# Attention, mixture of experts and a gated layer on one core: weight conversions taken off ScalarE, the closing of an expert from PSUM, twelve idle products for twenty-eight, and one more expert's weights loaded during attention

## The chip, the cores and the metric

The kernel runs on one core of one Trainium2 chip. Its time is the device time of one execution in microseconds; several executions are taken and their median is given. Engines are called as the profile calls them: TensorE (PE), VectorE (DVE), ScalarE (ACT), GpSimd (POOL) and SyncE (SP), which here does nothing but issue transfers.

## The reference

Three stages follow each other, with tokens as rows (1536 tokens, 512 columns).

```python
def _attn_ref(q, k, v):                 # (2, 8, 768, 64) each
    # every query sees keys at a distance under 16, and one summary key and value for each block of 32
    ...
def _moe_ref(x, w_skip, w_gate, w1, w2):      # 8 experts, 512 -> 1024 -> 512
    do_compute = x @ w_skip > 0               # the other tokens pass unchanged
    e_idx = np.argmax(xc @ w_gate, axis=1)    # one expert for each token
    ...
    h = np.maximum(xc[mask] @ w1[e], 0.0)
    y[mask] = gate_w[mask, None] * (h @ w2[e])
    out[do_compute] = xc + y
def _moe2_ref(x, w_in, w_out):                # 512 -> 2048 -> 512
    h = x @ w_in
    g = h * np.tanh(np.log1p(np.exp(h)))      # with a guard for h > 20
    return g @ w_out
```

The two weights of the last stage, `w_in` and `w_out`, arrive as 64-bit floats (two 32-bit words each) and are turned into 32-bit ones on the chip.

## The kernel before, in words

**Stages.** Attention runs over 24 groups of four 64-query tiles. In its last groups the gate's logits are summed, the tokens are ranked within their experts, and lists of row numbers are built. All token rows are written to `xd` in device memory; the last three stores of 512 KB come from `keep` (L775). Then follow the experts (L1077 to L1123), a branch for experts with many tokens that isn't taken with these inputs (L1136), and the last stage (from L1258), where TensorE alternates `up` (L989) and `down` (L1236) for 32 steps.

**Order.** The queues of SP and PE follow the order of the program text. On the other engines instructions stand in the order that a scheduler gave them, which in the expert loop and behind it is that of the text too.

**One expert.** GpSimd gathers up to 64 of its rows from `xd` (`fetch`, L855). The first product `g1_pair` (L892) puts the two halves of the hidden layer into partitions 0 to 63 and 64 to 127; ScalarE applies the relu; TensorE transposes the result (`flip`, L869); ScalarE copies it from PSUM (`hT`, L339); the second product `g2_pair` (L898) leaves two partial sums in one PSUM tile `yp`, again in the two halves of the partitions. The loop is staggered: the pass for expert e holds the first product of e and the second product of e - 1. `close_small` (L902) multiplies both halves by the gate and adds the token's row, and GpSimd writes the rows back to `xd` (`store`, L862). `yp` of these second products always comes from the same one of two PSUM buffers, since the branch for experts with over 64 tokens (`whole`, L1107) takes the other. So a second product can't begin before VectorE has closed the expert before. That branch is taken for experts 1 and 2.

**Weights of the experts.** Three sets of buffers are used in turn (`room`, L167): `big` for experts 0, 3 and 6, `raw` for 1, 4 and 7, `wb` (four buffers of `ring2`, which also held the values summed in attention) for 2 and 5. The loads of expert e + 2 stand in the pass of e, behind the second product of e - 1.

**Conversions.** `conv` (L118) turns one 128 x 512 piece of `w_in` or `w_out` into the two 32-bit parts that the last stage multiplies. ScalarE takes the absolute value of the high words (L127); six VectorE instructions follow (L129, L132, L135, L138, L113, L116). Ten of the 32 pieces are converted among the experts, `CONVS[e]` of them in the pass of e behind `close_small`; the tenth behind the branch at L1136. `conv_all` starts the next piece's ScalarE part while the present one is on VectorE, and the tile between them (`cv`) has two buffers. Four buffers hold raw pieces, so SP loads another when one has been converted.

**From the experts to the last stage.** After the last expert the rows are read back from `xd` in three transfers (`x_first`, L1125: 256, 512 and 768 KB), and they wait for the last store. TensorE meanwhile runs 28 products whose results nothing reads (`stir`, L1260); then it transposes the rows (`x_turn`, L1165), ScalarE rounds them (L1170), VectorE takes the remainder (L1171), and the last stage starts.

Of the kernel before, what the change touches and what calls it, by code (L numbers as in the profile page):

```python
# [15 lines left out]
ALU = mybir.AluOpType  # L16
# [12 lines left out]
def kernel(  # L29
# [87 lines left out]

    def conv(hi, low_, raw, hi_eng):  # L118
        t = cvp[0].tile([P, 512], F32, tag="cv", name="cv")
# [3 lines left out]
        else:  # L123
            words = raw.rearrange("p a b -> p (a b)").rearrange("p (f w) -> p f w", w=2)
            low, high = words.bitcast(U32)[:, :, 0], words.bitcast(U32)[:, :, 1]
            tu = t.bitcast(U32)
            nc.scalar.activation(out=t, in_=words[:, :, 1], func=AF.Abs)  # L127
            yield
            nc.vector.tensor_scalar(out=t, in0=t, scalar1=_f32(0x38000000), scalar2=_f32(0x47EFFFFF),  # L129
# [515 lines left out]
    LAG0 = N // 2 + 4  # L645
    RAW_AT = 17
    WAIT = [("w1", 0, kk) for kk in range(KD)] + [("w2", 0, kk) for kk in range(KD)]
    WAIT += [("w1", 1, kk) for kk in range(KD)] + [("w2", 1, kk) for kk in range(KD)]
    FEED_AT = dict(zip((7, 8, 10, 11, 13, 14, 16, 17), (2, 1) * 4))
    for i in range(-4, N - 3):  # L650
# [71 lines left out]
        if i == RAW_AT:  # L722
# [3 lines left out]
            spool.append(rctx.enter_context(tc.tile_pool(name="rawp", bufs=4, side="right", reuse_waits="tile")))  # L726
        if i >= RAW_AT + 3 and WAIT:
            load(WAIT.pop(0))
# [172 lines left out]
    def close_small(e, yp):  # L901
        gt, xt = gtl[0:HT, 0, e:e + 1], xtile[e]  # L902
        yo = mo.tile([P, DM], F32, tag="yo", name="yo")[0:HT]
        nc.vector.scalar_tensor_tensor(out=xt[0:HT], in0=yp[0:HT], scalar=gt, in1=xt[0:HT], op0=ALU.mult, op1=ALU.add)  # L904
        nc.scalar.copy(yo, yp[HT:P])  # L905
        nc.vector.scalar_tensor_tensor(out=yo, in0=yo, scalar=gt, in1=xt[0:HT], op0=ALU.mult, op1=ALU.add)
        store(first_ids(e), yo)
# [110 lines left out]
    def conv_all():  # L1018
        begun = []

        def begin():
            key = SEQ[len(begun)]
            gen = conv(*seat(key), raws[key], nc.vector)
            if WIDE:
                next(gen)
            begun.append((key, gen))

        for n in range(len(SEQ)):
            if n == len(begun):
                begin()  # L1030
            key, gen = begun[n]
            for at, _ in enumerate(gen):
                yield False
                if at == 2 and n + 1 < len(SEQ) and SEQ[n + 1] in raws and SEQ[n + 1] != ("out", NH):
                    begin()
            raws.pop(key)
            if n >= EARLY:
                load_next()
            yield True
# [20 lines left out]
    for _ in range(NCVR - 1):  # L1060
        load_next()
    for nm in ("w1", "w2"):
        for kk in range(KD):
            load((nm, 2, kk))
    for e in range(2, E):
# [12 lines left out]
    done = 0  # L1078
    CONVS = (0, 1, 2, 2, 1, 1, 1, 1)
    for e in range(E):  # L1080
# [39 lines left out]
    yp = acc_y()  # L1120
    g2_pair(E - 1, hT, yp)
    close_small(E - 1, yp)
    def x_loads(dst, s, c):  # L1123
# [10 lines left out]

    x_first()
    with tc.If(regs[E] > CUT):  # L1136
        enroll()
# [15 lines left out]
        x_first()  # L1153
    for _ in range(EARLY - done):
        go_conv()
    mctx.close()
# [101 lines left out]
    stir = fps.tile([P, 512], F32, tag="acc0", name="stir", bufs=1)  # L1258
    for _ in range(28):
        nc.tensor.matmul(stir, wi[0, 0][:, 0, 0, 0:P], wi[0, 0][:, 0, 0, :], start=True, stop=True)  # L1260
    xs[0] = [h_[:, c, :] for h_ in holds for c in range(CB)]
# [10 lines left out]
    for c, tag in enumerate(("acc4", "acc5", "h")):  # L1272
        x_halves(x_turn(xs[0][c], tag), xts[0], c)
    rest = list(enumerate(("h", "acc2", "acc3"), 3))
# [76 lines left out]
```

## Time and profile before

| | us |
|---|---|
| median of three runs | 529.85 |
| the three runs | 533.31, 527.6, 529.85 |
| profiled execution, its own time | 530.17 |
| profiled execution, span | 527.9 |
| TensorE busy | 479.5 (91%) |
| VectorE busy | 328.9 (62%) |
| ScalarE busy | 294.1 (56%) |
| GpSimd busy | 78.1 (15%) |

Times in the profile count from the span's start. Attention takes up to about 120 us, the experts run from 124.57 to 237.66, and the first product of the last stage that runs on without a longer pause starts at 251.73. A row of the timeline gives the start, the duration, the engine, the line and the operation with the tile that it writes and those that it reads; in brackets stands how long the engine had been idle and what ended that. `PEclk` is the granted clock of TensorE, 1.00 for 2.4 GHz and 0.50 for 1.2 GHz.

### The profile page before, as it was taken

Reading aid. Unit: us, or ns where it says so; the run is one execution under the profiler, and the core shown is the slowest. Engines: PE = TensorE matmul, PEld = TensorE weight load, DVE = VectorE, ACT = ScalarE, POOL = GpSimd, SP = SyncE. Lnnn points to the kernel's source line nnn. Section 1 sums busy time; section 2 is a strip of 40 time slices with the busy share of each in tenths; the row PEclk is TensorE's granted clock in tenths of the full one; section 3 lists DMA queues with packets and bytes.
Section 4 is the critical chain, followed back from the end, with each engine's and each line's share of the span. In section 5 each row is a group of like instructions: output and inputs, shape, how many; then the busy total and the mean of one; then the engine's idle time right before and its main releaser. Section 6 shows DMA issues by size and latency. Waiting matters only on the chain.

```text
span 527.9 us, 7985 instructions
## 1 busy us (share of the span) xinstructions
PE 479.5 (91%) x2818; PEld 377.3 (71%) x2818; DVE 328.9 (62%) x811; ACT 294.1 (56%) x477; POOL 78.1 (15%) x122
## 2 busy tenths in 40 slices
PE   4888979876999969967899999999999999999996
PEld 2777968762344323325898989999899998989985
DVE  3776847755012375563489888987888878454434
ACT  2687958520122132322597786866767677585660
POOL 5765532306211211100000000000000000000000
PEclk9999979876999998997999999999999999999999
DMA  8899999456998469943041221212212100030003
GB/s 182 220 215 213 232 243 296 127 195 208 371 400 305 174 225 402 389 177 126 1 160 44 78 69 51 79 45 76 77 44 81 40 1 0 1 119 1 1 0 119
DMA packets 58146, 76.41 MB, mean 145 GB/s; under 512 B 23950, under 2 KB 36286, under 8 KB 57712
## 3 DMA queue, kind: packets, MB, share of 16 engines
q1 hardware_dynamic: 56432, 73.95, 44.4%
q0 software_dynamic: 1664, 1.83, 1.2%
q8 instruction: 26, 0.43, 0.3%
q14 instruction: 24, 0.20, 0.1%
HBM read 70.76 MB, written 7.96 MB: 149 GB/s over the span
## 4 chain that ended last, share of the span: by engine, by line
PE 48%; DVE 4%; ACT 2%; issue 0%; DVEq 0%; ACTq 0%
PE acc L1236 23%; PE hp L989 22%; PE stir L1260 2%; PE ptx L1165 1%; DVE big L1228 1%; DVE big L1217 1%; DVE xt L1171 0%; DVE big L1205 0%; ACT big L1213 0%; DVE big L1225 0%; ACT big L1209 0%; ACT big L1202 0%; DVE wo L116 0%; DVE cv L135 0%; DVE ot L1251 0%
## 5 line engine op out<-in xcount | busy, mean ns | idle before, releaser
L989 PE MATMUL hp<-xt,wi 128*128 128x384 f32 x768 | 140.1, 336 | 2.4 <-ACT xt L1170 1.6
L989 PEld LDWEIGHTS hp<-xt,wi 128*128 128x128 f32 x768 | 134.5, 188 | 5.6 <-ACT xt L1170 2.0
L1236 PE MATMUL acc<-wo,big 128*128 128x512 f32 x576 | 138.2, 392 | 0.0
L1236 PEld LDWEIGHTS acc<-wo,big 128*128 128x128 f32 x576 | 107.2, 188 | 20.9
L1202 ACT ACTIVATE big<-hp 128x384 f32<-128x384 f32 x64 | 31.3, 492 | 65.7 <-PE hp L989 65.6
L1217 DVE TENSOR_TENSOR big<-big 128x768 f32<-128x768 f32 x32 | 30.6, 957 | 33.6 <-ACT big L1213 33.6
L1205 DVE COPY big<-hp 128x384 f32<-128x384 f32 x64 | 35.5, 556 | 23.3 <-ACT big L1202 23.3
L1213 ACT ACT_TABLE_LOAD x32 | 41.1, 1283 | 0.6
L1202 ACT ACT_TABLE_LOAD x31 | 39.8, 1283 | 0.6
L1228 DVE TENSOR_TENSOR big<-big 128x768 fp32r<-128x768 f32 x32 | 30.7, 959 | 3.1
L413 ACT ACTIVATE pr<-pr,nb 128x120 f32<-128x120 f32 x96 | 30.0, 386 | 1.1 <-DVE nb L407 0.9
L1213 ACT ACTIVATE big<-big,turn 128x768 f32<-128x768 f32 x32 | 30.1, 940 | 0.4
L917 DVE SCALAR_TENSOR_TENSOR yo<-yp,gtl,xs 128x512 f32<-128x512 f32 x2 | 1.5, 751 | 46.0 <-PE yp L929 46.0
L391 PE MATMUL sps<-kw,qb 128*128 128x120 f32 x192 | 28.2, 294 | 2.0 <-DVE qb L341 1.4
L391 PEld LDWEIGHTS sps<-kw,qb 128*128 128x128 f32 x192 | 25.8, 209 | 3.4 <-issue 2.4
L437 PE MATMUL xp<-vw,pts 120*64 120x65 f32 x384 | 21.2, 249 | 7.2 <-POOL vw L105 7.1
L1209 ACT ACTIVATE big<-big 128x768 f32<-128x768 f32 x32 | 27.1, 847 | 1.0
L127 ACT ACTIVATE cv<-raw 128x512 f32<-128x512 f32 x32 | 21.1, 663 | 9.8 <-DVE wi L116 7.3
L437 PEld LDWEIGHTS xp<-vw,pts 120*64 120x64 f32 x384 | 17.1, 153 | 11.1 <-POOL vw L105 8.1
L905 ACT COPY yo<-yp 64x512 f32<-64x512 f32 x8 | 4.7, 582 | 36.2 <-DVE xr L904 36.2
L424 ACT COPY pts<-tp 120x512 f32<-120x512 f32 x23 | 13.5, 585 | 18.2 <-PE tp L419 18.0
L135 DVE SCALAR_TENSOR_TENSOR cv<-raw,cv 128x512 uint32<-128x512 uint32 x32 | 22.2, 693 | 1.1
(182 smaller groups left out, 656.5 us busy)
## 6 DMA issues: line engine op xcount, KB each, us to landing
big<-in_moe_w_dram SPq DMA_DIRECT2D x24, 512.0 KB, 8.6
raw<-in_moe_w_dram SPq DMA_DIRECT2D x24, 512.0 KB, 8.3
raw<-in_moe_w_in_dram SPq DMA_DIRECT2D x16, 512.0 KB, 3.6
wb<-in_moe_w_dram SPq DMA_DIRECT2D x16, 512.0 KB, 8.0
raw<-in_moe_w_out_dram SPq DMA_DIRECT2D x16, 512.0 KB, 3.3
vw<-in_v_dram SPq DMA_DIRECT2D x16, 240.0 KB, 7.8
kr<-in_k_dram SPq DMA_DIRECT2D x16, 192.0 KB, 3.3
qr<-in_q_dram SPq DMA_DIRECT2D x16, 192.0 KB, 4.6
```

Of the source, the lines that this page charges most:

```text
L135: nc.vector.scalar_tensor_tensor(out=tu, in0=low, scalar=29, in1=tu, op0=ALU.logical_shift_right, op1=ALU.bitwise_or)
L391: nc.tensor.matmul(sps[:, j, :], qb[:, t].rearrange("p h i -> p (h i)"), kw[:, t, 0:NK], start=True, stop=True)
L413: nc.scalar.activation(out=pr[:, j, :], in_=pr[:, j, :], func=AF.Exp, bias=nb[:, j:j + 1], scale=SCALE)
L437: nc.tensor.matmul(xv[o0:o0 + QT, j // 2, h, :], pt[:, j, h * QT:(h + 1) * QT], vw[:, t, h, VP - D - 1:VP], start=True, stop=True)
L989: last_up[0] = nc.tensor.matmul(ps_, l(a), r(b_), start=(kk == 0 and n == 0), stop=(kk == KD - 1 and n == 2))
L1202: nc.scalar.activation(out=part(ds[n], half), in_=hps[n, half], func=AF.Sigmoid, scale=-1.0)
L1205: nc.vector.tensor_copy(part(us[n], half), hps.pop((n, half)))
L1209: nc.scalar.activation(out=d, in_=d, func=AF.Arctan)
L1213: nc.scalar.activation(out=d, in_=d, func=AF.Sin, scale=-2.0, bias=turn2)
L1217: nc.vector.tensor_tensor(out=u, in0=u, in1=part(ds[n], half), op=ALU.mult)
L1228: nc.vector.tensor_tensor(out=g_part(n, 1, half), in0=part(us[n], half), in1=g_part(n, 0, half).bitcast(F32), op=ALU.subtract)
L1236: nc.tensor.matmul(accs[t], g[:, a, t * P:(t + 1) * P], wo[f // 2][:, b_, f % 2, :], start=(n in FIRST and m == 0), stop=(n in LAST and m ...
```

## The change

1. `conv` gets a parameter `apart_`. Without it (the first ten pieces) the sign bit is cleared by one more VectorE instruction in place of ScalarE's; the next piece isn't started early. The other 22 pieces are converted as before.
2. `CONVS` becomes (0, 2, 2, 2, 1, 1, 1, 0). The tenth piece's instructions up to its rounding stand ahead of the last `close_small`, its last one behind it and ahead of the branch.
3. `close_small` reads the second half of `yp` from PSUM in its VectorE instruction; ScalarE's copy goes.
4. `stir`: 8 products, and 4 more behind the first transposes, for 28.
5. The eight loads of expert 2 join the list `WAIT` of loads in attention. That list is emptied faster: 1, 2, 3 and 4 loads at the ends of groups 17 to 20, where one stood at group 20; the buffers of `raw` open two groups earlier. What is left goes behind the three last stores to `xd`.

```diff
-    def conv(hi, low_, raw, hi_eng):
+    def conv(hi, low_, raw, hi_eng, apart_):
...
-            nc.scalar.activation(out=t, in_=words[:, :, 1], func=AF.Abs)
-            yield
+            if apart_:
+                nc.scalar.activation(out=t, in_=words[:, :, 1], func=AF.Abs)
+                yield
+            else:
+                nc.vector.tensor_scalar(out=tu, in0=high, scalar1=0x7FFFFFFF, scalar2=None, op0=ALU.bitwise_and)
...
-    RAW_AT = 17
+    RAW_AT = 15
...
+    WAIT += [("w1", 2, kk) for kk in range(KD)] + [("w2", 2, kk) for kk in range(KD)]
...
-        if i >= RAW_AT + 3 and WAIT:
+        for _ in range(max(0, i - RAW_AT - 1)):
             load(WAIT.pop(0))
...
-        nc.scalar.copy(yo, yp[HT:P])
-        nc.vector.scalar_tensor_tensor(out=yo, in0=yo, scalar=gt, in1=xt[0:HT], op0=ALU.mult, op1=ALU.add)
+        nc.vector.scalar_tensor_tensor(out=yo, in0=yp[HT:P], scalar=gt, in1=xt[0:HT], op0=ALU.mult, op1=ALU.add)
...
-            gen = conv(*seat(key), raws[key], nc.vector)
-            if WIDE:
+            gen = conv(*seat(key), raws[key], nc.vector, len(begun) >= EARLY)
+            if WIDE and len(begun) >= EARLY:
                 next(gen)
...
-                if at == 2 and n + 1 < len(SEQ) and SEQ[n + 1] in raws and SEQ[n + 1] != ("out", NH):
+                if at == 2 and EARLY <= n + 1 < len(SEQ) and SEQ[n + 1] in raws and SEQ[n + 1] != ("out", NH):
...
-    for nm in ("w1", "w2"):
-        for kk in range(KD):
-            load((nm, 2, kk))
...
-    CONVS = (0, 1, 2, 2, 1, 1, 1, 1)
+    CONVS = (0, 2, 2, 2, 1, 1, 1, 0)
...
     g2_pair(E - 1, hT, yp)
+    run(cv, 4)
     close_small(E - 1, yp)
...
     x_first()
+    go_conv()
...
-    for _ in range(EARLY - done):
-        go_conv()
...
-    for _ in range(28):
-        nc.tensor.matmul(stir, wi[0, 0][:, 0, 0, 0:P], wi[0, 0][:, 0, 0, :], start=True, stop=True)
+    def stir_on(n):
+        for _ in range(n):
+            nc.tensor.matmul(stir, wi[0, 0][:, 0, 0, 0:P], wi[0, 0][:, 0, 0, :], start=True, stop=True)
+
+    stir_on(8)
...
-        x_halves(x_turn(xs[0][c], tag), xts[0], c)
+        pt = x_turn(xs[0][c], tag)
+        if c == 0:
+            stir_on(4)
+        x_halves(pt, xts[0], c)
```

Three places show how instructions move. First ScalarE from the closing of expert 1, at the end of the pass of expert 2, on (the `hT` there is what the second product of expert 2 multiplies, in the pass of expert 3), before:

```order
130 L1107 UNCONDITIONAL_BRANCH x2
131 L905 COPY yo<-yp 64x512
132 L127 ACTIVATE cv<-raw 128x512 x2
133 L339 COPY hT<-pt 128x512
134 L885 ACTIVATE hr<-hp 128x512
135 L339 COPY xT<-pt 128x256
```

and with the change, at the same place:

```order
128 L1107 UNCONDITIONAL_BRANCH x2
129 L342 COPY hT<-pt 128x512
130 L889 ACTIVATE hr<-hp 128x512
131 L342 COPY xT<-pt 128x256
132 L1073 TENSOR_LOAD cnti
133 L1107 COMPARE_AND_BRANCH
```

Behind the branch `hT` now comes first; the copy `yo` and the two absolute values `cv` are gone from ahead of it.

Second, VectorE at the closing of the last two experts, up to the branch (`xr` and `yo` are the closing, `cv` and `wo` a conversion), before:

```order
498 L904 SCALAR_TENSOR_TENSOR xr<-yp,gtl,xr 64x512
499 L906 SCALAR_TENSOR_TENSOR yo<-yo,gtl,xr 64x512
500 L129 TENSOR_SCALAR cv<-cv 128x512
501 L132 TENSOR_SCALAR cv<-cv 128x512
502 L135 SCALAR_TENSOR_TENSOR cv<-raw,cv 128x512
503 L138 SCALAR_TENSOR_TENSOR cv<-raw,cv 128x512
504 L113 CAST wo<-cv 128x512
505 L116 TENSOR_TENSOR wo<-cv,wo 128x512
506 L904 SCALAR_TENSOR_TENSOR xr<-yp,gtl,xr 64x512
507 L906 SCALAR_TENSOR_TENSOR yo<-yo,gtl,xr 64x512
508 L1136 COMPARE_AND_BRANCH
```

and with the change:

```order
513 L908 SCALAR_TENSOR_TENSOR xr<-yp,gtl,xr 64x512
514 L909 SCALAR_TENSOR_TENSOR yo<-yp,gtl,xr 64x512
515 L131 TENSOR_SCALAR cv<-raw 128x512
516 L132 TENSOR_SCALAR cv<-cv 128x512
517 L135 TENSOR_SCALAR cv<-cv 128x512
518 L138 SCALAR_TENSOR_TENSOR cv<-raw,cv 128x512
519 L141 SCALAR_TENSOR_TENSOR cv<-raw,cv 128x512
520 L113 CAST wo<-cv 128x512
521 L908 SCALAR_TENSOR_TENSOR xr<-yp,gtl,xr 64x512
522 L909 SCALAR_TENSOR_TENSOR yo<-yp,gtl,xr 64x512
523 L116 TENSOR_TENSOR wo<-cv,wo 128x512
524 L1138 COMPARE_AND_BRANCH
```

The conversion has one instruction more and its last one stands behind the last closing; before, another whole conversion followed behind the branch.

Third, SP's queue at the end of attention (`vw` are values of attention, `raw` and `wb` the weights of experts 1 and 2, `xd<-xb` the last three stores of rows), before:

```order
84 L292 DMA vw_121<-in_v_dram 96x10x64
85 L293 DMA vw_121<-in_v_dram 80x64
86 L294 DMA vw_121<-in_v_dram 80x64
87 L199 DMA raw<-in_moe_w_dram 128x2x512
88 L775 DMA xd<-xb_117 128x2x512 x3
89 L199 DMA raw<-in_moe_w_dram 128x2x512 x3
90 L199 DMA raw<-in_moe_w_in_dram 128x1024 x4
91 L199 DMA wb<-in_moe_w_dram 128x1024 x4
92 L199 DMA wb<-in_moe_w_dram 128x2x512 x4
```

and with the change:

```order
85 L295 DMA vw_121<-in_v_dram 96x10x64
86 L296 DMA vw_121<-in_v_dram 80x64
87 L297 DMA vw_121<-in_v_dram 80x64
88 L202 DMA raw<-in_moe_w_dram 128x2x512 x3
89 L202 DMA wb<-in_moe_w_dram 128x1024 x4
90 L202 DMA wb<-in_moe_w_dram 128x2x512 x2
91 L779 DMA xd<-xb_117 128x2x512 x3
92 L202 DMA wb<-in_moe_w_dram 128x2x512 x2
93 L202 DMA raw<-in_moe_w_in_dram 128x1024 x4
```

Nine loads of 512 KB now stand between the last values and the three stores, where one stood.

## Rows read from the trace of the kernel before

**Rows 1.** The page: gigabytes per second in 40 slices of 13.2 us.
```profile
GB/s 182 220 215 213 232 243 296 127 195 208 371 400 305 174 225 402 389 177 126 1 160 44 78 69 51 79 45 76 77 44 81 40 1 0 1 119 1 1 0 119
```

**Rows 2.** Stretches: length, busy us of PE, PEld, DVE, ACT, POOL; PEclk, DMA share, GB/s.
```profile
97.00:109.00 12.00, 10.06 (x104) 9.01 (x103) 7.24 (x44) 5.27 (x14) 0.56 (x2) 0.64 0.26 67
199.50:203.60 4.10, 4.10 (x12) 0.98 (x8) 0.79 (x2) 0.00 (x0) 0.00 (x0) 0.59 1.02 417
240.30:243.80 3.50, 3.50 (x8) 2.78 (x9) 3.31 (x6) 1.19 (x2) 0.00 (x0) 0.50 0.64 203
300.00:350.00 50.00, 50.00 (x258) 45.40 (x256) 43.74 (x73) 38.41 (x47) 0.00 (x0) 1.00 0.21 71
```

**Rows 3.** Timeline, passes of experts 2 to 7: start, us, engine, line, tiles, [idle before].
```profile
155.19 1.94 PE L892 MATMUL hp<-wb,xT 128*64 128x512 f32 x8
...
181.49 0.66 PE L869 MATMUL pt<-ident,hr 128*128 128x128 f32 x4
...
186.12 0.67 ACT L127 ACTIVATE cv<-raw 128x512 f32<-128x512 f32 x1 [3.66 <-DVE wi L116]
...
187.46 3.65 PE L898 MATMUL yp<-wb,hT 128*64 128x512 f32 x16 [3.05 <-ACT hT L339]
...
198.25 5.35 PE L898 MATMUL yp<-big,hT 128*64 128x512 f32 x16 [2.02 <-ACT hT L339]
...
221.31 1.94 PE L892 MATMUL hp<-raw,xT 128*64 128x512 f32 x8 [0.31 <-PEq L1107]
```

**Rows 4.** Timeline, VectorE in the pass of expert 2: closing, then a conversion.
```profile
180.40 0.73 DVE L904 SCALAR_TENSOR_TENSOR xr<-yp,gtl,xr 64x512 f32<-64x512 f32 x1
...
182.57 0.41 DVE L129 TENSOR_SCALAR cv<-cv 128x512 f32<-128x512 f32 x1
...
185.40 0.69 DVE L116 TENSOR_TENSOR wi<-cv,wi 128x512 fp32r<-128x512 f32 x1
186.00 0.42 DVE L129 TENSOR_SCALAR cv<-cv 128x512 f32<-128x512 f32 x1
```

**Rows 5.** Timeline from the closing of expert 6 to the last stage.
```profile
229.92 0.74 DVE L904 SCALAR_TENSOR_TENSOR xr<-yp,gtl,xr 64x512 f32<-64x512 f32 x1 [3.18 <-PE yp L898]
...
230.59 3.65 PE L898 MATMUL yp<-raw,hT 128*64 128x512 f32 x16 [0.72 <-PEq L1107]
...
235.53 0.74 DVE L904 SCALAR_TENSOR_TENSOR xr<-yp,gtl,xr 64x512 f32<-64x512 f32 x1
...
236.92 0.74 DVE L906 SCALAR_TENSOR_TENSOR yo<-yo,gtl,xr 64x512 f32<-64x512 f32 x1 [0.65 <-ACT yo L905]
237.94 0.90 POOL L862 DMA_INDIRECT xd<-yo,idl  x1 [4.58 <-DVE yo L906]
...
240.22 2.18 SPq L1125 DMA_DIRECT2D big<-xd  x3
240.25 0.43 DVE L129 TENSOR_SCALAR cv<-cv 128x512 f32<-128x512 f32 x1 [2.59 <-DVEq L1136]
...
240.30 8.27 PE L1260 MATMUL stir<-wi 128*128 128x512 f32 x28 [6.06 <-DVEq L1136]
...
248.41 1.48 PE L1165 MATMUL ptx<-ident,big 128*128 128x128 f32 x12
...
251.73 1.14 PE L989 MATMUL hp<-xt,wi 128*128 128x384 f32 x5 [0.51 <-DVE xt L1171]
```

**Rows 6.** Transfers by line: KB each, median us from issue to landing.
```profile
big<-xd SPq DMA_DIRECT2D x1, 768.0 KB, 6.6
...
big<-xd SPq DMA_DIRECT2D x1, 256.0 KB, 3.1
```

**Rows 7.** Timeline, end of attention: SP's issues and the first gather.
```profile
97.29 0.43 SPq L199 DMA_DIRECT2D raw<-in_moe_w_dram  x1
...
109.23 3.96 SPq L775 DMA_DIRECT2D xd<-xb  x3
...
120.68 1.05 POOL L855 DMA_INDIRECT xr<-xd,idl  x1 [23.11 <-DVE gtp L581]
```

## The prediction

> **What bounds the kernel now.** I read the stretches first, then the timeline from the experts to the last stage. In the last stage TensorE is busy 50.00 of 50 us at a clock of 1.00 [rows 2], and the chain of waits from 251.73 on runs mostly through TensorE: what comes earlier there ends earlier, one for one. The questions are therefore when TensorE begins that stage and what held it back. Three places do. Twice a second product of an expert waits for `hT`: 3.05 us at 187.46 and 2.02 us at 198.25 [rows 3]. The transposes for the first wait had ended at 181.49 + 0.66 = 182.15; ScalarE was held at 186.12 by an absolute value that waited 3.66 us for VectorE to free a `cv` buffer, and `hT` stood behind it in the queue. The product at 198.25 then took 5.35 us where its like at 187.46 took 3.65, since the clock fell (0.59 in that stretch) [rows 2, 3]. Third, between the last second product's end, 230.59 + 3.65 = 234.24, and the last stage at 251.73 lie 17.5 us: closing, store, branch, 28 idle products of 8.27 us, transposes [rows 5]. The eight products in 240.30 to 243.80 ran at 0.50 [rows 2]; 28 cost 8.27, so the other 20 took about 4.8.
>
> **Experts.** The waits go with ScalarE's part: 3.05 + 2.02 = 5.07. Without the pauses I expect the clock not to fall there: 5.35 - 3.65 = 1.70. Together 6.77. ScalarE's copy of `yo` (the 0.65 us that VectorE waited at 236.92 [rows 5]) also leaves every closing; only the last lies on the path.
>
> In exchange VectorE gets longer. A conversion takes 186.00 - 182.57 = 3.43 us [rows 4]. The new instruction isn't in this trace: the nearest rows are a one-source instruction at 0.41 and a two-source one at 0.69 [rows 4]. It has one source and a constant, so I take 0.41, with its gap 0.45, and 0.69 as upper end. Two conversions become 7.76 us. What is late next is the closing, and behind it the next second product, which needs `yp`. The closing of expert 1 starts at 180.40; two dependent instructions of about 0.74 and the follow-on gap bring the conversions to 181.85 and their end to 189.6. Then come a count's load and a branch on VectorE; TensorE paid 0.72 us for both at 230.59 [rows 5], which I take, and the upper end is the 2.59 that VectorE spent at the far branch [rows 5]. Closing of expert 2: 190.3 to 191.8; TensorE wants `yp` at 198.25 - 5.07 = 193.2. Again two conversions and a branch: closing of expert 3 ends at 201.7. Without waits the two second products lie 198.25 - 187.46 - 2.02 = 8.8 apart [rows 3], so TensorE wants `yp` again at 202.0. That fits by a hair; I charge 0.3. **Experts: -6.5.**
>
> The freed DMA time gains nothing by itself: the first product of expert 2 started at 155.19 behind the product before it, with no wait for weights [rows 3]. Later loads follow their buffers, so they move up with TensorE, and SP's raw pieces wait for conversions as before. From the end of expert 2's second product, 187.46 - 3.05 + 3.65 = 188.1, until the last piece of expert 7's first weights 9.4 MB must arrive (18 pieces). At 389 GB/s, one of the fullest slices among the experts [rows 1], that takes 24.2 us, till 212.3; the product wants its first piece at 221.31 - 6.5 = 214.8 [rows 3]. Just covered; no charge.
>
> **Attention.** Nine loads (4.7 MB) now go out from 97.3 on [rows 7], in 12 us whose DMA share was 0.26 [rows 2]. They land beside work that needs no transfer. The three stores at 109.23 stand behind them, and the first gather at 120.68 needs both the stores and VectorE's lists [rows 7]. At 389 GB/s nine loads take 12.1 us, so they are through at 109.4: charge 0, bounds 0 and +1.5. The trace has no store queued behind loads. The Trainium skill, "DMA: Bandwidth & Descriptors", section "Queues, rings and completion order", says that each DMA engine takes the descriptors of one ring in order. By that the stores wait for the whole rest of the loads, which at 389 GB/s is next to nothing; no row here shows it. What a low rate would do is a rival below.
>
> **Closing.** Let expert 6's second product end at 229.9, as before. VectorE closes it, 229.92 to 231.4. The tenth conversion's first six instructions take 0.45 and 185.40 - 182.57 = 2.83 [rows 4]: until 234.6, just later than TensorE's 234.24. The last closing then runs without ScalarE, to 236.1; before it ended at 236.92 + 0.74 = 237.66 [rows 5]. So the store goes 1.5 us earlier (1.25 if the new instruction takes 0.69). The rows' transfers started 2.28 behind the store (237.94 to 240.22): now 238.7. The rest of the conversion, 0.69 [rows 4], now stands ahead of the branch: end 236.8. The branch took 2.59 from VectorE's last end to 240.25, and `stir` started right behind it [rows 5]; now 239.4. That is 0.9 earlier than 240.30, not 1.5.
>
> **Idle products.** Eight at the low clock, 0.43 each as in 240.30 to 243.80 [rows 2], end at 242.85. The first rows are there at 238.7 + 3.1 = 241.8; if they needed the 6.6 us of the large transfer [rows 6], 245.3, so this is bounded by +2.5. The transposes start 5.55 earlier than at 248.41. From there to 251.73 it took 3.3 us [rows 5]; the four products (0.21 each at the full clock) delay the second and third transposes and so ScalarE, 0.6. **Closing and idle products: -5.55 + 0.6 = -5.0.** The bulk of it is the 4.8 us of products at the full clock; it holds if the full clock has come by the time the eight are through.
>
> **Sum.** 530.17 - 6.5 - 5.0 = **518.7 us**. The profiled execution stands 0.3 above the median of 529.85, and the three runs spread over 5.7, so I don't correct for that.
>
> **Rivals.**
>
> *VectorE becomes the bound among the experts.* For it: the hair above, and a branch price that the trace doesn't show for a late VectorE. At 0.69 and 2.59 the conversions end at 190.1, the closing of expert 2 at 194.2 (+1.0), the one of expert 3 at 206.5, 3.5 behind TensorE. Against it: TensorE paid only 0.72. It costs up to 4.5: 519 to 522.9.
>
> *The clock doesn't hold.* With fewer products the low clock may reach into the last stage, or fall again while TensorE waits for ScalarE and VectorE, now about 1.7 us in one piece. For it: after a wait of 2.02 it fell at 199.5. Against it: after 3.05 at 187.46 it didn't, nor in the pauses before 251.73. One stretch of 3.5 us at 0.50, as at 240.30 [rows 2], loses 1.7, two lose 3.5: 520.4 to 522.2. The Trainium skill, "TensorE: Matmul & The Clock Gate", section "HAM oscillation", says that waits between bursts let the clock fall, so that every burst starts low. By that rule both prices fall due, 522.2; the trace agrees only after some of its waits, so this rival has no more than its chance.
>
> *The loads hold back the gathers.* In attention the busy slices moved 182 to 243 GB/s [rows 1]. Loads and stores are 6.3 MB from 97.3 on. At 243 they end at 123.2, the first gather is 3 us late: 521 to 522. At 182 they end at 131.9, 11.2 later than 120.68, and the gain is gone but for 0.3. Below 181 the change is **slower**; that is the point which decides. At 127, the lowest slice there, they end at 146.9: 530 to 545. Against it: those slices were full of small pieces, while weights alone moved at 371 and more.
>
> *The waits turn into waits for weights.* The cover of 2.5 us at expert 7 is thin; at 305 GB/s, the slower slice there [rows 1], the last piece comes at 218.9, 4.1 late: up to 522.8. Against it: the pieces come and are wanted one by one, and that slice held pauses of the queue.
>
> *It doesn't do what it says.* If `hT` is late for a reason other than ScalarE's queue, only the -5.0 is left: 525.2, within 1%. Little speaks for it, since the absolute value ends and `hT` starts 0.03 later.
>
> **How the numbers follow.** Forecast 0.48, VectorE 0.16, clock 0.14, gathers a little late 0.07 and so late that it gets slower 0.04, weights 0.06, not as said 0.05. Own range of the forecast: 516 to 521.5. The range of 515 to 524.5 takes in the rivals except the last of the gathers and of "not as said", and a run's scatter below. A measurement of this kernel can tell about 1% from no change, so faster means under 524.55: the first three, the late gathers and the weights, 0.91, less 0.06 for two of them at once: 0.85. Slower by over 1% (gathers at under 158 GB/s): 0.03. Within: 0.12.
>
> **What would show it.** In the changed profile the second products of experts 2 and 3 start right behind TensorE's work, without a wait for ScalarE; VectorE's closing of expert 3 ends about when TensorE needs it; the first gather still starts near 120.7; the last store leaves 8 us earlier than at 237.94; eight `stir` products run at 0.50 and the four later ones at 1.00; the steady stretch of the last stage begins near 240.2. Wrong would be: a late first gather, a wait of a second product for VectorE of more than 1 us, a clock of 0.50 behind the transposes, or a wait for rows.

## The result, and the profile after

The changed kernel took 527.11 us (median of 20 runs, 519.33 to 532.21), the kernel before 531.51 on the same chip (20 runs): ratio 0.9899, interval 0.9865 to 0.9933. That is 5.4 us or 1% faster, where 11.5 us were forecast. Ratios below leave disturbed runs out, so they can differ a little from the quotient of two medians. The profiled execution took 527.98, span 526.2; the changed kernel was profiled twice more, as f4 and k3 below.

First the experts. The rows of after that answer to [rows 3] (timeline, TensorE):

```profile
138.05 5.35 PE L902 MATMUL yp<-big,hT 128*64 128x512 f32 x16 [1.89 <-issue]
...
188.63 3.65 PE L902 MATMUL yp<-wb,hT 128*64 128x512 f32 x16
197.33 3.65 PE L902 MATMUL yp<-big,hT 128*64 128x512 f32 x16
...
218.99 2.27 PE L896 MATMUL hp<-raw,xT 128*64 128x512 f32 x8 [0.61 <-DMA raw<-in_moe_w_dram]
```

Both waits for ScalarE are gone, and the product that took 5.35 takes 3.65; the clock of 200 to 225 rose from 0.94 to 1.00. But there is a new wait for weights at expert 7, and a wait early on, at 138.05, that no step spoke of. VectorE in the pass of expert 2, after (answers to [rows 4]):

```profile
186.28 0.41 DVE L131 TENSOR_SCALAR cv<-raw 128x512 uint32<-128x512 uint32 x1
...
194.51 0.74 DVE L908 SCALAR_TENSOR_TENSOR xr<-yp,gtl,xr 64x512 f32<-64x512 f32 x1
```

The new instruction takes 0.41. Two conversions fill 186.28 to 194.37 (8.09 us, where the prediction took 7.76), the closing follows 0.14 later and ends before TensorE wants it at 197.33.

The end of the experts, after (answers to [rows 5]), and two rows of SP's waits (what waited <- what released it, us in total, times, longest), of after and then, by itself, of before:

```profile
228.79 3.65 PE L902 MATMUL yp<-raw,hT 128*64 128x512 f32 x16 [0.76 <-PEq L1107]
...
234.95 1.11 POOL L866 DMA_INDIRECT xd<-yo,idl  x1 [4.00 <-DVE yo L909]
236.60 1.28 ACT L1271 ACT_TABLE_LOAD   x1 [4.27 <-ACTq L1138]
237.84 1.54 SPq L1126 DMA_DIRECT2D big<-xd  x3
...
238.09 3.57 PE L1262 MATMUL stir<-wi 128*128 128x512 f32 x8 [5.64 <-ACT warm L1271]
243.69 0.66 PE L1165 MATMUL ptx<-ident,big 128*128 128x128 f32 x4 [2.03 <-SPq L1138]
...
248.00 2.69 PE L992 MATMUL hp<-xt,wi 128*128 128x384 f32 x6 [0.68 <-ACT xt L1170]
```

```profile
SPq L1138 <- SPq L1138: 4.2, 1, 4.2
```

```profile
SPq L1136 <- SPq L1136: 4.6, 1, 4.6
```

Counted from the start of the last second product, the store leaves at 6.16 us instead of 7.35 and the eight products start at 9.30 instead of 9.71. (What held them last, by their row, was ScalarE's first work behind the branch, `warm`, and not VectorE.) Then TensorE waits 2.03 us. Not for a transfer: for SP's branch (SPq L1138). SP issues the three row loads, 237.84 to 239.38, comes to the last branch and spends 4.2 us there; TensorE goes on at once (239.38 + 4.2 = 243.6). Before, the same row stood at 4.6: 242.40 + 4.6 = 247.0, and the 28 products lay over it until 248.57.

Stretches of after: length, busy us by engine, then PEclk, DMA share, GB/s.

```profile
234.30:241.60 7.30, 3.51 (x8) 2.49 (x8) 0.97 (x2) 1.49 (x2) 1.11 (x1) 0.53 0.52 158
241.80:244.80 3.00, 1.11 (x7) 1.03 (x8) 0.00 (x0) 0.29 (x1) 0.00 (x0) 0.99 0.73 246
244.90:251.20 6.30, 5.59 (x20) 4.40 (x19) 2.07 (x3) 1.36 (x3) 0.00 (x0) 0.50 0.01 3
```

The clock came to 1.00 when the eight products were through, and the first four transposes still ran at it (0.66). From 244.9 on it was 0.50 again, and the other transposes and the first groups ran so for 6.3 us. The last short wait ahead of the steady stage is this row, of after and then of before:

```profile
254.94 3.24 PE L992 MATMUL hp<-xt,wi 128*128 128x384 f32 x17 [0.28 <-DVE xt L1171]
```

```profile
256.64 2.52 PE L989 MATMUL hp<-xt,wi 128*128 128x384 f32 x13 [0.28 <-DVE xt L1171]
```

Cut at five rows of TensorE into four stretches, the profiles give (us; from the last of these rows to the end all take 271.0 to 271.3):

| stretch | before | after | f4 | k3 | e1 |
|---|---|---|---|---|---|
| expert 0's first product to expert 1's second | 35.33 | 39.28 | 35.28 | 40.06 | 35.39 |
| to expert 5's second | 57.44 | 50.54 | 50.54 | 50.53 | 50.53 |
| to expert 7's second | 13.25 | 14.06 | 13.95 | 14.75 | 14.43 |
| to the steady part of the last stage | 26.05 | 26.15 | 29.23 | 28.91 | 23.48 |

So the experts gave 6.9, expert 7's weights took back 0.7 to 1.5, and the end, where 5.0 were to come, gave nothing and took 0.1 to 3.2. The first line turned out to be no part of the change (below).

### The profile page after: what moved, and what is told of

Same layout as the page of the kernel before. It is cut to its first block, busy times and chain, and to the rows that moved or that the text cites. A ratio compares the mean times of both kernels' runs of the same rounds, so it can differ in the third digit from the quotient of the medians.

```text
span 526.2 us, 7944 instructions
## 1 busy us (share of the span) xinstructions
PE 481.5 (92%) x2802; PEld 378.3 (72%) x2802; DVE 335.1 (64%) x821; ACT 283.7 (54%) x459; POOL 78.9 (15%) x122
## 4 chain that ended last, share of the span: by engine, by line
PE 47%; DVE 3%; ACT 2%; issue 0%; DVEq 0%
PE acc L1236 23%; PE hp L992 23%; PE ptx L1165 1%; DVE big L1228 1%; DVE big L1217 1%; DVE big L1205 0%; ACT big L1213 0%; DVE big L1225 0%; ACT big L1209 0%; DVE cv L138 0%; ACT big L1202 0%; DVE wo L116 0%; DVE ot L1251 0%; ACT L1213 0%; ACT L1202 0%
## 5 line engine op out<-in xcount | busy, mean ns | idle before, releaser
L342 ACT COPY hT<-pt 128x512 f32<-128x512 f32 x10 | 5.9, 586 | 49.3 <-PE pt L873 43.2
L394 PE MATMUL sps<-kw,qb 128*128 128x120 f32 x192 | 29.8, 306 | 1.5 <-DVE qb L344 1.3
L394 PEld LDWEIGHTS sps<-kw,qb 128*128 128x128 f32 x192 | 27.3, 220 | 2.8 <-POOL kw L105 1.7
L138 DVE SCALAR_TENSOR_TENSOR cv<-raw,cv 128x512 uint32<-128x512 uint32 x32 | 22.1, 692 | 1.1
L141 DVE SCALAR_TENSOR_TENSOR cv<-raw,cv 128x512 uint32<-128x512 uint32 x32 | 21.9, 685 | 0.3
```

What stands on the lines that cost most here:

```text
L138: nc.vector.scalar_tensor_tensor(out=tu, in0=low, scalar=29, in1=tu, op0=ALU.logical_shift_right, op1=ALU.bitwise_or)
L394: nc.tensor.matmul(sps[:, j, :], qb[:, t].rearrange("p h i -> p (h i)"), kw[:, t, 0:NK], start=True, stop=True)
```

## The experiments

Each edit is against the kernel named; "rows behind the branch" is e1's edit. Kernels of one letter shared a chip and the runs of before. Single letters such as A, C or W are the theories named in the texts of what was expected, and "the end" is the last line of the table.

**e1: row loads behind the last branch.** Against the changed kernel:

```
-    x_first()
     go_conv()
     with tc.If(regs[E] > CUT):
         ...
-        x_first()
+    x_first()
```

> The changed kernel, but the three loads of the first rows stand once, behind the last branch (in the changed kernel they stand ahead of it and again inside it). Theory A: with the loads ahead of the branch, SP's skipped path waits for all three transfers (1.5 MB) before TensorE is let through, so the first transposes came 5.85 us after the loads (237.84 to 243.69). Behind the branch TensorE waits for the first 256 KB alone: the loads go 0 to 1.5 us later, and the first transposes start 3 to 3.5 us behind them, near 241.5 instead of 243.69; the time falls by 1 to 2.5 us against the changed kernel. Theory B: the first 256 KB itself needs 5.8 us because the three transfers share the queue: the first transposes stay 5.5 us or more behind the loads, at 244 or later, and the time is the same or longer by up to 1.5.

Ratio 0.982 (0.9777 to 0.9863). Timeline, and the 256 KB load's time to landing:

```profile
234.17 3.75 PE L1261 MATMUL stir<-wi 128*128 128x512 f32 x8 [6.53 <-DVEq L1137]
234.68 1.33 SPq L1126 DMA_DIRECT2D big<-xd  x3
237.72 1.05 PE L1164 MATMUL ptx<-ident,big 128*128 128x128 f32 x4
```

```profile
big<-xd SPq DMA_DIRECT2D x1, 256.0 KB, 2.8
```

The transposes follow the eight products without a wait, 3.04 behind the loads instead of 5.85, though the loads themselves go 1.6 later (10.69 behind the last second product, 9.05 in after). B falls. A's result is right, but its reason, a wait for all three transfers, is not: in the profile of after packets of the rows still ran until 245.0, when the transposes had been going since 243.69.

The rows themselves were there. In the five profiles of kernels with the loads ahead of the branch and a wait at the transposes that have the landing of the 256 KB (e3, f1, f4, e4, k3), it came 2.7 to 4.0 us behind its issue, and the transposes 6.9 to 7.5 behind it. f4, with its landing last:

```profile
228.65 1.32 SPq L1126 DMA_DIRECT2D big<-xd  x3
235.73 1.12 PE L1165 MATMUL ptx<-ident,big 128*128 128x128 f32 x4 [2.69 <-SPq L1138]
```

```profile
big<-xd SPq DMA_DIRECT2D x1, 256.0 KB, 3.3
```

**e2: 28 idle products again.** `stir_on(28)`, `stir_on(0)`.

> The changed kernel with 28 idle products ahead of the transposes and none between them, as in the kernel before. The prediction's step (20 products at the full clock are worth 4.7 us): 4 us longer than the changed kernel. Theory A (the rows are 5.85 us behind their loads, so 5.6 us of the 8.3 are hidden, and the transposes then run at the full clock): start 238.1, products end 246.4, the transposes and the first group at a clock of 1.00, the last stage's steady part within 0.5 us of the changed kernel; the time the same within 1 us.

0.9917 (0.9878 to 0.9955), not told apart from the changed kernel's 0.9899: no gain from taking 20 products away shows. The end took 27.92, within what the changed kernel's profiles show. Here SP was through the branch at 233.73 + 1.58 + 5.3 = 240.6 and the products ended at 243.8, so some 3 us of them lay open.

**e3: 17 idle products.** `stir_on(17)`.

> The changed kernel with 17 idle products ahead of the first transposes instead of 8. Theory A: 8 products at 0.43 and 9 at 0.24 fill 238.1 to 243.7, so TensorE has no wait for rows, and the clock is at 1.00 when the transposes come and stays there; the half-clock stretch of 244.6 to 251.5 goes, 2 to 2.5 us shorter than the changed kernel. Rival: the clock falls during the transposes all the same, because TensorE waits there for ScalarE and VectorE: same time as the changed kernel within 0.5 us.

0.9863 (0.9818 to 0.9907).

```profile
230.79 1.32 SPq L1126 DMA_DIRECT2D big<-xd  x3
231.04 5.52 PE L1262 MATMUL stir<-wi 128*128 128x512 f32 x17 [5.67 <-DVEq L1138]
237.69 0.66 PE L1165 MATMUL ptx<-ident,big 128*128 128x128 f32 x4 [1.13 <-SPq L1138]
```

```profile
234.10:246.60 12.50, 9.30 (x52) 7.22 (x50) 4.10 (x7) 3.82 (x7) 0.00 (x0) 1.00 0.20 71
```

The release came 6.90 behind the loads, so a wait of 1.13 was left, against the expectation; the clock stayed at 1.00 all the same. The end took 24.89, against 26.15 to 29.23. By the profiles seventeen products were the better choice with the loads where they stood; the times don't show it, for e4, with eight, has 0.9864 on the same chip.

**e4: the third expert's weights behind attention again** (part 5 undone).

> The changed kernel with part 5 undone: the third expert's weights are loaded behind attention again, RAW_AT 17. In the changed kernel expert 2's first product started 4.3 us later than before (159.47 against 155.19), behind a wait of 1.89 for ScalarE at 138.05, a fallen clock, and a start 0.34 later. Theory C (the early loads cause it): expert 2's first product starts near 155.2 again, no wait of ScalarE near 137, and the time falls by 2 to 4 us. Theory D (ScalarE's 6.1 us at its first branch has nothing to do with the loads and comes now and then): expert 2's first product is no earlier on the whole, and the time is the same within 1 us or longer.

0.9864 (0.9816 to 0.9911): not told apart from the changed kernel. Its profile has a wait of 3.00 for SP's branch and an end of 28.29. No late copy of `hT` here, but none in e1, e2 and e3 either.

**f1: part 4 alone, on the kernel before.** `stir_on(8)`, `stir_on(4)` for the 28.

> The kernel before with part 4 alone (8 idle products, 4 behind the first transposes; experts, closing and loads as before). The prediction's step: 4.1 us shorter (4.7 less 0.6), ratio 0.992. Theory A (the first transposes wait until all three row transfers are in, 5.85 to 6.9 us behind their start, and the clock falls in that wait): transposes at about 246.4 instead of 248.41 with a wait of 2 to 3 us ahead of them, then 0.50 for some us, the last stage's steady part within 1 us of before; ratio 0.998 to 1.004.

1.0054 (0.9968 to 1.0139).

```profile
236.64 3.65 PE L1262 MATMUL stir<-wi 128*128 128x512 f32 x8 [5.92 <-DVEq L1136]
244.16 1.12 PE L1165 MATMUL ptx<-ident,big 128*128 128x128 f32 x4 [3.87 <-SPq L1136]
```

```profile
SPq L1136 <- SPq L1136: 5.5, 1, 5.5
```

Alone, this part shows no gain: a wait of 3.87 in place of the products, then 0.50, and in this profile an end of 29.58 against 26.05. I had expected it within 1 us.

**f2: rows behind the branch, parts 1 to 3 undone.** `conv(..., True)`, the old `CONVS`, ScalarE's copy, no `run(cv, 4)`, `go_conv()` behind the branch.

> The kernel of e1_rows_after_branch with parts 1 to 3 undone: absolute values on ScalarE in every conversion, closings with ScalarE's copy, the tenth conversion in its old place, the old table of conversions. Against e1 it shows what parts 1 to 3 are worth alone. The prediction's steps (6.5 among experts and 0.9 at the end): 7 us longer than e1 (518.85 with 528.26 for before), ratio 0.994 to 0.998. Rival, that most of the experts' gain is given back behind (weights that come late at expert 7): under 4 us longer than e1, ratio under 0.990.

0.995 (0.9905 to 0.9995), 0.013 or 6.9 us above e1, as the prediction's steps had it; the two intervals, from two chips, leave some 3 us either way. Its profile has both waits again:

```profile
182.77 3.65 PE L902 MATMUL yp<-wb,hT 128*64 128x512 f32 x16 [3.04 <-ACT hT L342]
...
193.56 5.35 PE L902 MATMUL yp<-big,hT 128*64 128x512 f32 x16 [2.02 <-ACT hT L342]
```

**f3: rows behind the branch, TensorE kept warm.** 24 products into an `acc_h()` tile ahead of `tc.If`, `stir_on(14)` behind it.

> The kernel of e1_rows_after_branch with 24 idle products right behind the last second product, ahead of the branch, and 14 behind it instead of 8. In e1 TensorE lay idle for 6.5 us there (227.64 to 234.17), the clock fell to 0.50 at 232.9 and rose at 239.4. If the pause is what costs the clock: 1.00 from the last second product to the last stage, the 14 products take 3.0 instead of 3.75 for 8, the transposes start as soon as the rows are in, at most 0.3 earlier, and run at once at 1.00: 1 to 1.5 us shorter than e1. Rival (the pause at the branch itself, about 1 to 2 us, is enough to lower the clock, or the products delay TensorE's own branch): the same as e1 or up to 1 us longer.

0.9839 (0.9781 to 0.9897), as e1.

```profile
225.00:246.00 21.00, 17.25 (x84) 12.72 (x81) 7.76 (x13) 5.78 (x10) 1.10 (x1) 1.00 0.41 139
```

The clock held, 1.00 for 21 us. It bought nothing: the end took 23.63 (e1: 23.48), since the loads went 4.56 behind the store and the transposes another 3.77 behind them. With the rows this late, the clock isn't what TensorE waits for.

**f4: the changed kernel again.**

> The changed kernel once more, for its time and a second profile on the chip of the three others. Theory A: transposes 5.85 us or more behind the start of the row loads, a wait of about 2 us for them, 0.50 behind; ratio 0.990. Theory D (ScalarE's late copy at 137.41 in the first profile, 4 us, comes now and then): no such wait in this profile, the first product of expert 2 about 34 us behind the first product of expert 0 instead of 34.6, or 30.6 as before.

0.9948 (0.9899 to 0.9998); no late copy. Stretches of the eight products and of what came behind the wait:

```profile
229.30:233.00 3.70, 3.70 (x8) 2.44 (x8) 0.00 (x0) 0.00 (x0) 0.00 (x0) 0.50 0.87 277
235.70:245.00 9.30, 8.56 (x29) 7.17 (x30) 2.08 (x3) 2.24 (x4) 0.00 (x0) 0.50 0.01 4
```

Here 0.50 lasted 9.3 us behind the wait, 3 us more than in the first profile: the two ends of 26.15 and 29.23.

**g1: e1 with the tenth conversion behind the branch.** No `run(cv, 4)`; `go_conv()` behind `x_first()`.

> The kernel of e1_rows_after_branch with only the tenth conversion put back behind the last branch, as before (the experts' conversions and the sum from PSUM stay). It tells what setting the tenth conversion round the last closing is worth. The prediction's step (0.9 of the store's 1.5 us reach the idle products): stir starts 0.9 later behind the last second product than in e1, 11.1 against 10.18. Rival (what releases stir is the branch of VectorE, and that took 2.5 to 2.6 us in the kernels with the old order, 2.8 to 4.3 in those with the new one, whatever ended ahead of it): stir starts at 9.0 to 9.6 us behind the last second product, the branch takes 2.5 to 2.7, and the time is the same as e1's or up to 1 us shorter.

0.9821 (0.9773 to 0.987), as e1. The idle products started 9.40 behind the last second product, earlier than e1's 10.18, not later: no gain from setting the conversion round the last closing shows. But the branch was not shorter: VectorE ended at 5.22, so 4.18 passed. My guess about its price was wrong as well.

**g2: e1 with the raw pieces behind each expert's second weights.** The `while ... load_next()` moved behind the loop over `w2`.

> The kernel of e1_rows_after_branch with the raw pieces of the last stage's weights loaded behind each expert's second weights instead of between its two. In e1 SP stood behind a raw piece that waited for VectorE from 184.15 to 188.4, the transfers' share was 0.14 to 0.58 from 179 to 191, and the first product of expert 7 then waited 0.97 us for weights; between the second products of experts 5 and 7 lay 1.0 us more than with the old conversions. Theory W (SP held by the raw pieces makes the weights late): no wait for weights at expert 7, that stretch 0.7 to 1.2 us shorter. Rival (the transfers themselves, 9.4 MB at about 400 GB/s, are the limit whatever the order): the wait stays at 0.5 to 1.4 us. A third way: the raw pieces come late now and a second product waits for a closing behind VectorE, up to 2 us longer.

0.9776 (0.9718 to 0.9834), the lowest of all, within e1's interval. The wait it was meant to take away is still there, so W, with the raw pieces as the cause, falls:

```profile
215.48 2.27 PE L896 MATMUL hp<-raw,xT 128*64 128x512 f32 x8 [1.05 <-DMA raw<-in_moe_w_dram]
```

SP now stood behind expert 5's weights, whose buffers came free late (170.59 to 190.26). In 184 to 196 the transfers moved 193 GB/s, and 398 to 406 from there to 216; in e1, a microsecond earlier, it was 200 and then 399 to 402.

**g3: g2 and f3 together.** `range(26)`, `stir_on(10)`.

> The kernel of g2_raw_behind_weights with 26 idle products ahead of the last branch and 10 behind it (f3_warm_over_branch had 24 and 14). If all holds: 1.00 from the experts to the end, no wait for weights at expert 7, transposes as soon as the rows are in: 0.5 to 1.5 us shorter than g2, ratio to before near 0.979. If the branches take the gain (ScalarE's took 6.4 instead of 4.4 us in f3): the same as g2.

0.9833 (0.9785 to 0.9881): nothing gained over g2, and 2.54 us of waiting for weights at expert 7.

**h1 to h4: loads early or late, and the transfers beside the branch.** h1 is e1 with part 5 undone, h2 is e1, h3 is e1 with the last four `load_next()` behind `x_first()`, h4 is the kernel before with part 5.

> The kernel of e1_rows_after_branch with part 5 undone (third expert's weights behind attention). Theory C (the early loads make ScalarE's copy behind its first branch late in some executions): no such wait here, and 1 to 3 us shorter than h2 on this chip. Theory D (it comes on some chips, whatever the loads): the same as h2 within 1 us, the wait as likely here as there. Theory E (the early loads help, the weights of expert 7 come sooner): 1 us or more longer than h2, the wait for weights at expert 7 over 1.4 us.

> The kernel of e1_rows_after_branch once more, beside the three others on one chip. Expected: ratio 0.982 to before. Theory C: in its profile the copy of hT may come late; theory D: it comes late here exactly if it does in h1 and h4.

> The kernel of e1_rows_after_branch with the last four raw pieces loaded behind the first rows, so that no transfer runs when the engines take the last branch. Theory K (the branch is long because the engines' code is fetched beside those transfers): VectorE's branch takes 2.5 to 2.6 us again, ScalarE's less than the 4.3 of e1, idle products start at 9.0 or less behind the last second product instead of 10.18, 1 us shorter, as far as the conversions of the last stage don't come late. Rival (the branch's price has nothing to do with transfers): idle products start at 9.8 to 10.7 as in e1; the same or longer by up to 2 us if the conversions of the last stage now come late.

> The kernel before with part 5 alone. The prediction charged it nothing: ratio 0.997 to 1.003. Theory C: 0.5 to 3 us longer in those executions in which ScalarE's copy comes late, ratio 1.001 to 1.006. Theory D: the same.

Ratios 0.9824 (0.9771 to 0.9876), 0.9834 (0.9783 to 0.9885), 0.9803 (0.9754 to 0.9853), 0.9994 (0.9959 to 1.0029). Early or late loads make no difference, with the old experts or the new. ScalarE idled 5.46, 4.97, 4.87 and 3.71 us ahead of its first `hT` here, with and without early loads, against 2.67 in the kernel before and in all eight profiles of e and f. In g and k it was 5.5 to 8.2. C falls. So does the chip as a reason, for e and h ran on the same one.

In h3 the branch got shorter. ScalarE's first work behind it, in h2 and then in h3, and h3's idle products and first transposes:

```profile
231.11 1.28 ACT L1270 ACT_TABLE_LOAD   x1 [4.41 <-ACTq L1137]
```

```profile
228.77 1.28 ACT L1270 ACT_TABLE_LOAD   x1 [2.98 <-DVE yo L909]
...
236.17 3.75 PE L1261 MATMUL stir<-wi 128*128 128x512 f32 x8 [4.76 <-DVEq L1135]
...
240.73 1.12 PE L1164 MATMUL ptx<-ident,big 128*128 128x128 f32 x4 [0.81 <-DMA big<-xd]
```

VectorE's branch took 1.89 (236.17 less its end at 234.28) against 3.70 in h2, and the products started 8.41 behind the last second product against 10.13. That speaks for K; for ScalarE it is mixed with an absolute value that h3 moves too. The end of h3 was no shorter (23.81, h2 22.56). Its loads, which wait for the store, went 4.09 behind it; the transposes came only 0.7 earlier, at 12.97 behind the last second product against 13.68, and then ran at the low clock (the first four took 1.12, in h2 0.60).

**k1: one row load ahead of the branch, two behind.**

> The changed kernel with only the first of the three row loads (256 KB) ahead of the last branch, the other two behind it. Theory F (SP's skip of the branch waits for its code, which comes beside the rows' transfers): with 256 KB the skip is shorter, 2.5 to 3.5 us instead of 4.2 to 5.6, the first transposes 4 to 5 us behind the load instead of 5.9 to 7.5. Theory G (SP's skip takes 4 to 5.6 us by itself): the wait of SP at the branch stays over 4.2, first transposes 5.5 or more behind the load, and the second transposes come 2 us later still. Time: F 0.5 to 2 us shorter than k3, G the same or longer.

0.9807 (0.9734 to 0.9879).

```profile
SPq L1140 <- SPq L1140: 3.5, 1, 3.5
```

With 256 KB beside it SP's branch took 3.5 us instead of 4.2 to 5.7 with 1.5 MB, and the transposes came 4.17 behind the load. That speaks for F; it is one reading, and SP issued one load ahead of the branch instead of three. The second transposes then waited 2.18 for their rows.

**k2: e1, g2 and h3 together; k3: the changed kernel.**

> The changed kernel with all three of: row loads behind the branch, raw pieces behind each expert's second weights, and the last four raw pieces behind the rows. If each keeps what it showed alone: ratio 0.976 to 0.980, 3 to 8 us shorter than k3. Rival: the stretches don't add up, since the store's landing sets the rows whatever the branch does: ratio 0.980 to 0.984, as e1.

> The changed kernel a third time, beside the two others. Expected: ratio 0.988 to 0.996; SP's wait at the branch 4.2 to 5.6 us, the first transposes 0.1 to 0.2 behind it; the steady part of the last stage 26 to 29 us behind the last second product.

0.9801 (0.9741 to 0.986) and 0.9867 (0.9809 to 0.9926). The gains don't add up: the eight kernels with the rows behind the branch and the new experts lie between 0.978 and 0.984, the changed kernel at 0.990, 0.995 and 0.987. e1 is the smallest edit that gets there. Against the changed kernel on one chip only f3 and f4 have intervals apart; the other pairs overlap.

## Why the prediction was wrong, step by step

**Experts, -6.5: right.** The stretch that holds both waits and the low clock fell by 6.90, in three profiles of the changed kernel. Its parts are 3.05, 2.02 and 1.70, with the 0.3 for VectorE not charged: the closing of expert 2 ended 1.1 us ahead of its need and that of expert 3 0.2 (205.82 against 206.03), the hair that was forecast. f2 against e1 shows 6.9 as time too; that the figures are equal is luck, given the intervals. The rival of VectorE as the bound found no wait for it.

**Weights, "just covered; no charge": mis-sized by 0.7 to 1.5.** The first product of expert 7 waited 0.5 to 1.4 us and ran a little slower. The term took 389 GB/s from the end of expert 2's second product on. In the profile of after the transfers moved 203 GB/s from 188 to 200, and 397 to 401 only from there to 222. g2 shows much the same with the raw pieces elsewhere in SP's queue, so their place alone isn't the reason. The rival had the place, at little more than a third of its price, but not its rate: 305 GB/s is the slice of 158 to 171, and the slices of this stretch had 225, 402 and 389 [rows 1].

**Attention, 0: right.** h4 alone 0.9994, h1 against h2 the same. The first gather came at 121.11, with attention 0.4 later as a whole.

**Closing, -0.9: not there.** The store left 1.19 earlier, near the 1.5. But the branch price of 2.59, read once, was taken as fixed, and the new order paid 2.8 to 4.8 (1.7 and 1.9 in k2 and h3, without transfers). Idle products started 0.4 us earlier in the first profile, 0.7 and 0.3 later in the other two; g1, too, shows no gain from the place of the conversion.

**Idle products, -4.65 (the -5.55 less the closing's 0.9) + 0.6: the step that failed.** It said that the first rows are there at 241.8, by the landing of the 256 KB transfer [rows 6], with +2.5 as bound for the large one. Neither row was the price, and that the bound puts the transposes at 245.3, near the sum below, is luck. TensorE's first transposes stand behind SP's branch, and the trace of before had that in a view that it did not use: SP waiting 4.6 us at L1136, until 247.0. Of 8.27 us of products, 1.5 lay open. The row to subtract from was not TensorE's busy time but the next thing behind it.

By that row the transposes start at 238.7 + 2.18 + 4.6 = 245.5, 2.9 earlier than before; and then a second loss comes due. From the transposes to the steady part the kernel before took 8.23, the changed one 11.25: 3.0 more, most of it at a clock of 0.50. The four later products are 1.3 of it, where 0.6 was charged. The rest, 1.7, is the rival "the clock doesn't hold", at its price of 1.7 to 3.5, with a cause it did not have: the wait for the branch. 2.9 against 3.0 leaves nothing, and 530.17 - 6.5 + 0.8 = 524.5, 5.7 under before, is near the 5.4 measured. In part this is luck: f4 and k3 took 12.4 from the transposes to the steady part, which would leave a gain of some 3 us, and the three ratios of the changed kernel (0.9899, 0.9948, 0.9867) scatter as widely. The page that the prediction weighed there, the Trainium skill, "TensorE: Matmul & The Clock Gate", section "HAM oscillation", pointed the right way: behind waits of 2.03 to 3.87 that followed eight products the transposes ran at 0.50 (in the first profile all but the first four); behind 1.13 that followed seventeen they ran at 1.00. Waits of under 1 us behind eight products went both ways: after 0.94 in f2 the clock was 1.00, after 0.81 in h3 the first transposes took 1.12.

**What would show it:** second products without ScalarE, yes; closing of expert 3 in time, yes; store 8 us earlier, no (3.0 in the first profile, which has the late `hT` in it; in f4, counted from expert 0's first product, 7.45); four later products at 1.00, no; steady stage near 240.2, no; a wait ahead of the transposes (for SP's branch, not for the rows) and a clock of 0.50 behind it, the signs that it named for being wrong, both yes.

**Open.** The late `hT` behind ScalarE's first branch came in all kernels that ran together or in none, on one chip both ways. It added about 4 us to the first profile of the changed kernel (1.89 of waiting, and a product at the low clock) and isn't tied to the change, since h4 has it with the old experts and h1 with the late loads. The copy in the first profile of after and then in that of before:

```profile
137.41 0.58 ACT L342 COPY hT<-pt 128x512 f32<-128x512 f32 x1 [6.09 <-PE pt L879]
```

```profile
133.36 0.58 ACT L339 COPY hT<-pt 128x512 f32<-128x512 f32 x1 [2.67 <-PE pt L869]
```

The kernel before had medians of 527.98 and 528.26 beside e and f and of 531.51 to 536.15 beside the others, as if it were hit too, but no profile of it was taken there. What makes it isn't known.

## What to carry to other kernels

Before you shorten filler work, find what would release the engine without it: here the queue's own wait at a branch, one line in the waits of an engine that looked idle. A transfer issued ahead of a branch isn't usable when it lands, if the consumer also waits for the issuing engine to pass the branch; issue it behind the branch, or measure the branch. And where filler ends well before its successor can start, its loss can be paid twice, as here: as a wait and as a low clock.

## What the runs showed of the hardware

The skipped branch was far from free, and its price went with what the transfers did: SP's took 3.5 us beside 256 KB of rows and 4.2 to 5.7 beside 1.5 MB, VectorE's 1.7 to 1.9 with no weight transfers near it (h3, k2), 2.5 to 2.7 in the old order, where they had just ended, and 2.8 to 4.8 in the others, where most often their tail still ran (in e1 at shares of 0.41, 0.23 and 0.06 in 230 to 233). In five profiles (after, e3, e4, f1, f4) a packet of the instruction queue came 1.4 to 1.9 us ahead of TensorE's release; this is the one of after, in 242 to 243 (queue, packets, MB, share):

```profile
q14 instruction: 1, 0.01, 3.5%
```

That fits code that is fetched through the same engines as the rows. The Trainium skill, "Runtime: NRT & Kernel Launch", section "Instruction fetch mechanics", says that a taken branch to code outside the pages held must wait for a transfer of that code. The times agree with it; that this packet is SP's code, no run here shows.
